# Lightning attention into a SiLU FFN: hand-assigned staging buffers, a 512-column opening FFN, fewer TensorE instructions, and chunks 6 and 7 attended later

## The chip, the cores and the metric

The kernel runs on one core of a Trainium2 chip. The metric is the device time of one execution in microseconds (us). The median of five runs is compared between two versions of the kernel; the profile shows one execution, whose own time is given below. The engines are named PE or TensorE (matmul; its weight loads are shown apart as PEld), DVE or VectorE, ACT or ScalarE, POOL or GpSimd, and SP or SyncE. SyncE issues nearly all DMAs (loads, stores and DMA transposes) from one queue, in the order of the program. TensorE accumulates in PSUM. A tile in PSUM comes from one of four kinds of buffers that the program calls tags: att (3 buffers), h (2), o (2) and kv (1).

## The reference

Inputs are q, k and v of shape (4, 8, 768, 64): four sequences, eight heads, 768 tokens, head size 64; a decay lam per head; and two FFN matrices, w_in (512 x 2048) and w_out (2048 x 512). All are float32. For each head the attention works on blocks of tokens:

```python
intra = (qb @ kb^T) * Dmask            # lam ** (i - j) for i >= j, else 0
out[block] = intra @ vb + (qb * lam ** (pos + 1)) @ kv_state
kv_state = lam ** block * kv_state + (kb * lam ** (block - 1 - pos))^T @ vb
```

The result, seen as 3072 tokens by 512, goes through the FFN:

```python
h = x @ w_in
out = (h / (1 + exp(-h))) @ w_out
```

There is no softmax, so the decay can be split into a factor on q and one on k or v. The output is 3072 x 512 in float32.

## The kernel before, in words

**Tiling.** The 3072 tokens are 24 chunks of 128 tokens, six to a sequence. Matmul operands are bf16. Chunks form ten FFN groups (GROUPS, line 17): five of 256 tokens, four of 384, one of 256. For a chunk c the steps are: scale q and k by the decay; transpose both so that the head dimension lies on partitions; "s", the scores of keys against queries, followed by the causal mask on VectorE (op_m at line 292 for the first chunks, masked at line 479 for the others); "d", the update of the running state kv in PSUM, which is then copied to SBUF as kvbd (copy_kv, line 455); "o", the output from masked scores and values plus state and queries, copied to xt on ScalarE (op_x, line 315; st_o, line 511). When all chunks of a group are in xt, the first FFN matmul runs from xt and w_in into h_ps (lines 529 and 552), ScalarE applies SiLU and writes g, and the second FFN matmul runs from g and w_out into o_ps (line 578). VectorE copies o_ps to ob (line 582) and SyncE stores it (line 570).

**The opening.** Chunks 0 to 3 are handled in pairs (0 and 1, 2 and 3) by a list written out by hand, ORDER (line 25). Each word is a step with its arguments: qc, kc and vc cast and scale half a of the heads (line 257); tq and tk transpose on TensorE (line 264); qt and kt copy the transposes out of PSUM (line 274); s, m, d, kv, o and x are the steps named above; w casts half of a w_in piece; u and g are matmuls and SiLU of the first FFN for groups 0 and 1; wl loads ScalarE's function table; z issues matmuls on a tile of zeros (line 638). The last letter of a word is the engine: D for VectorE, A for ScalarE, P for POOL. Groups 0 and 1 are computed apart, with matmuls of 256 columns; the tokens of a pair are interleaved in xt, and the store of these groups undoes it (line 586).

**Staging.** LOADS (line 23) is the order in which SyncE issues the first loads: halves of K, Q and V of the chunk pairs, then all of w_in. Raw q, k and v pairs and w_out pieces rotate through a pool of six buffers called pair; w_in pieces go through the pools kf, vf and qf, as sixteen transfers of 256 KB (line 161), and are all issued ahead of any cast.

**After the opening.** Lines 674 to 710 mix the second FFN of groups 0 and 1 (down0) with attention of chunks 4 and 5. next_prep (line 662) takes the next chunk: it scales q and k on POOL (lines 356 and 350), issues two DMA transposes on SyncE (qt and kn, lines 373 and 374), and issues the three loads of the chunk two further on (line 232). spread_k copies kn into the block-diagonal tile ktbd on VectorE, spread_v copies the values into vpad (line 387). clear_halves (line 196) zeroes two of these tiles each with four memsets on POOL.

**The stretches.** From group 2 on, stretch (line 745) merges lists of steps by a fractional place: ups(g), the first FFN of group g, spans 0 to 1; pieces(g+1), the attention steps s, d, o of the next group's chunks, spans a given interval; downs(g-1), the second FFN of the group before, likewise. The sorted order is the program order on all engines. Engines run their own instructions in this order and wait for one another by semaphores.

## Time and profile before

| | |
|---|---|
| median of five runs | 217.7 us (216.54 to 220.94) |
| the profiled execution's own time | 216.54 us |
| its span, first to last instruction | 214.8 us |
| TensorE busy | 204.2 us, 95% |
| VectorE busy | 117.5 us, 55% |
| ScalarE busy | 98.5 us, 46% |
| POOL busy | 53.4 us, 25% |
| attention of chunks 0 to 3, until the first FFN matmul | 18.7 us |
| end of the first FFN of groups 0 and 1 | 33.7 us |
| start of group 2's first FFN | 50.9 us |
| mean DMA share, 5 to 60 us / 60 to 105 us / 105 to 155 us | 0.99 / 1.04 / 0.88 |

How to read the lines that follow. A row of a timeline is: start in us from the span's first instruction, time in us of the run of like instructions, engine, line of the kernel, operation, output tile <- input tiles, shape, count, and in brackets the idle time of the engine just before, with what ended it. SPq is SyncE's queue; its rows show the issuing of a transfer, and the landing comes later. Matmuls overlap in the records, so the start-to-start spacing is what one costs: 109 ns at 256 columns and 216 ns at 512. A DMA share is the mean busy share of sixteen DMA engines; it can exceed one where packets queue.

### The profile page before, as it was taken

What the parts mean: (1) busy time and instruction counts of PE and PEld (TensorE: products, weight loads), DVE (VectorE), ACT (ScalarE), POOL (GpSimd) and SP (SyncE); (2) the same over time, 40 slices, a digit from 0 to 9 for tenths busy, and PEclk for the clock granted to TensorE, in tenths of its full rate; (3) what the DMA queues carried; (4) which work ended last, traced back from release to release, by engine and by line L of the source; (5) the groups of instructions that cost most, each with busy time, mean ns of one, the idle gap of its engine ahead of it and who ended that gap; (6) DMA issues with size and microseconds to landing.
All of it is one profiled execution on the core that took longest, in us unless ns stands there. A gap on an engine that the chain in (4) does not pass through costs nothing.

```text
span 214.8 us, 4591 instructions
## 1 busy us (share of the span) xinstructions
PE 204.2 (95%) x1808; PEld 135.7 (63%) x1831; DVE 117.5 (55%) x263; ACT 98.5 (46%) x186; POOL 53.4 (25%) x66
## 2 busy tenths in 40 slices
PE   7878999998699999999999999999999999999994
PEld 5666885565676787766665656556655565566654
DVE  3786447696875599854856785446471352100121
ACT  3983763325362655445555445435445333423210
POOL 6360002539433324323333332222100000000000
PEclk9999999999999999999999999999999999999999
DMA  4999999988899999999999999868411011011112
GB/s 114 332 380 360 371 400 220 318 199 174 214 278 197 228 200 204 176 209 158 194 235 233 226 199 188 200 177 173 123 49 52 2 49 53 0 49 49 52 49 98
DMA packets 95670, 38.58 MB, mean 180 GB/s; under 512 B 81056, under 2 KB 88608, under 8 KB 95648
## 3 DMA queue, kind: packets, MB, share of 16 engines
q1 hardware_dynamic: 95504, 38.29, 71.3%
q8 instruction: 14, 0.23, 0.4%
q14 instruction: 8, 0.07, 0.1%
q10 hardware_dynamic: 144, 0.00, 0.0%
HBM read 27.27 MB, written 6.29 MB: 156 GB/s over the span
## 4 chain that ended last, share of the span: by engine, by line
PE 70%; DMA 14%; SPq 9%; POOL 3%; issue 2%; DVE 1%; DVEq 0%; POOLq 0%
PE o_ps L578 30%; PE h_ps L552 19%; PE h_ps L529 11%; DMA pair<-in_moe_w_out_dram 5%; PE op L507 4%; SPq L224 4%; SPq L232 3%; PE sp L476 3%; DMA vf<-in_moe_w_in_dram 3%; DMA qf<-in_moe_w_in_dram 3%; DMA qf<-in_q_dram 2%; DMA kn<-kb 2%; PE o_part L595 2%; PE kv_ps L452 1%; SPq L161 1%
## 5 line engine op out<-in xcount | busy, mean ns | idle before, releaser
L578 PE MATMUL o_ps<-w_out_bf,g 128*128 128x512 bf16 x345 | 87.8, 379 | 1.2
L578 PEld LDWEIGHTS <-g 128*128 128x128 bf16 x368 | 35.0, 98 | 30.8
L556 ACT ACTIVATE g<-h_ps 128x384 bf16<-128x384 f32 x64 | 31.4, 491 | 46.6 <-PE h_ps L552 46.1
L552 PE MATMUL h_ps<-xt,w_in_bf 128*128 128x384 bf16 x256 | 50.6, 326 | 0.0
L529 PE MATMUL h_ps<-xt,w_in_bf 128*128 128x256 bf16 x384 | 47.2, 273 | 0.7 <-ACT w_in_bf L179 0.7
L534 ACT ACTIVATE g<-h_ps 128x512 bf16<-128x512 f32 x48 | 27.8, 596 | 34.3 <-PE h_ps L529 34.1
L529 PEld LDWEIGHTS <-w_in_bf 128*128 128x128 bf16 x384 | 36.4, 98 | 7.9 <-ACT w_in_bf L179 1.1
L582 DVE COPY ob<-o_ps 128x512 f32<-128x512 f32 x23 | 15.9, 691 | 40.8 <-PE o_ps L578 40.6
L356 POOL TENSOR_TENSOR qb<-qf,lam_fwd 128x512 bf16<-128x512 f32 x18 | 18.9, 1051 | 68.3 <-DMA qf<-in_q_dram 65.0
L552 PEld LDWEIGHTS <-w_in_bf 128*128 128x128 bf16 x256 | 23.7, 98 | 17.2
L483 DVE TENSOR_TENSOR ss<-sp,mask 128x512 bf16<-128x512 f32 (+1 forms) x40 | 21.0, 566 | 12.9 <-PE sp L476 12.6
L387 DVE COPY vpad<-vb 64x256 bf16<-64x256 bf16 x72 | 25.5, 354 | 1.6
L350 POOL TENSOR_TENSOR kb<-kf,lam_bwd 128x512 bf16<-128x512 f32 x20 | 20.9, 1046 | 1.5 <-DMA kf<-in_k_dram 1.4
L183 DVE COPY ktbd<-kn 64x512 bf16<-64x512 bf16 x36 | 14.7, 408 | 10.6 <-DMA kn<-kb 10.3
L183 DVE CAST kvbd<-kv_ps 64x256 bf16<-64x256 f32 x32 | 13.5, 421 | 9.5 <-PE kv_ps L452 9.1
L515 ACT ACTIVATE xt<-op 128x512 bf16<-128x512 f32 x20 | 11.9, 597 | 11.1 <-PE op L507 10.4
L476 PEld LDWEIGHTS <-ktbd 128*128 128x128 bf16 x160 | 9.3, 98 | 6.7 <-DVE ktbd L183 3.8
L476 PE MATMUL sp<-qt,ktbd 128*128 128x128 bf16 (+1 forms) x160 | 10.3, 207 | 2.9 <-DVE ktbd L183 2.9
L179 ACT ACTIVATE vb<-vf 128x512 bf16<-128x512 f32 x18 | 11.2, 622 | 0.0
L507 PE MATMUL op<-ss,vpad 128*128 128x128 bf16 (+1 forms) x160 | 10.3, 207 | 0.0
L507 PEld LDWEIGHTS <-vpad 128*128 128x128 bf16 x160 | 8.9, 98 | 0.3
L183 DVE CAST w_out_bf<-pair 128x1024 bf16<-128x1024 f32 x7 | 5.4, 770 | 5.5 <-DMA pair<-in_moe_w_out_dram 5.5
(83 smaller groups left out, 121.6 us busy)
## 6 DMA issues: line engine op xcount, KB each, us to landing
out_dram<-ob SPq DMA_DIRECT2D x23, 256.0 KB, 3.4
kf<-in_k_dram SPq DMA_DIRECT2D x20, 256.0 KB, 4.0
vf<-in_v_dram SPq DMA_DIRECT2D x20, 256.0 KB, 4.5
qf<-in_q_dram SPq DMA_DIRECT2D x18, 256.0 KB, 3.5
pair<-in_moe_w_out_dram SPq DMA_DIRECT2D x8, 512.0 KB, 8.6
kf<-in_moe_w_in_dram SPq DMA_DIRECT2D x6, 256.0 KB, 5.3
vf<-in_moe_w_in_dram SPq DMA_DIRECT2D x6, 256.0 KB, 5.4
pair<-in_k_dram SPq DMA_DIRECT2D x4, 256.0 KB, 4.5
```

The lines of the kernel that those rows point to most:

```text
L183: nc.vector.tensor_copy(dst, src)
L350: VG[e].tensor_tensor(kb, rawk.pop(c).rearrange("s (p j) d -> s p j d", j=2), decay(lam_bwd, c % NB), op=AL.mult)
L356: nc.gpsimd.tensor_tensor(qb, rawq.pop(c).rearrange("s (p j) d -> s p j d", j=2), decay(lam_fwd, c % NB), op=AL.mult)
L387: nc.vector.tensor_copy(vh[64 * j:64 * j + 64, :, h, j, :], vb[64 * h:64 * h + 64, :, j, :])
L476: nc.tensor.matmul(sp[:, p, :], lhsT=lhsT, rhs=qt[:, p, a:], start=True, stop=True)
L483: VG[e].tensor_tensor(ss, sp, m[:, None, :n].to_broadcast([128, 4, n]), op=AL.mult)
L507: nc.tensor.matmul(dst, lhsT=lhsT, rhs=rhs, start=(i == 0), stop=(i >= len(terms) - NP), skip_group_check=True)
L529: nc.tensor.matmul(hps[g, i][:, a:a + 256], lhsT=w_in_bf[:, ko, m * 128:(m + 1) * 128], rhs=xt[g][:, ko, :], start=(ko == 0 and u == 0), s ...
L534: nc.scalar.activation(gg.rearrange("p u n -> p (u n)"), hps[g, i], AF.Silu)
L552: nc.tensor.matmul(hp[:, a:z], lhsT=w_in_bf[:, ko, m * 128:(m + 1) * 128], rhs=xt[g][:, ko, a:z], start=(ko == 0 and a == 0), stop=(ko == ...
L556: nc.scalar.activation(gg, hp[:, :n], AF.Silu)
L578: nc.tensor.matmul(o, lhsT=gt[g, ko][:, mt * BLK:(mt + 1) * BLK], rhs=w_out_bf[:, ko, :], start=(ko == 0), stop=(ko == KO_OUT - 1))
```

## The change

- **Staging.** Six constant tiles of 512 KB (pairs) are handed out in turn by next_pair, to the K, Q and V pairs of chunks 0 to 3, then to w_in pieces 0 to 5, w_out pieces 0 to 5, q of chunk 4 and w_out pieces 6 and 7. A w_in piece is now one transfer of 512 KB, issued once the casts that read the tile's former content are in the program (the list later); pieces 6 and 7 go through kf and vf. Loads of chunks 4 to 7 are issued after the casts of w_out 0 to 5.
- **Opening order.** ORDER is rewritten: several copies and casts change engines, steps of the second pair are split by halves of the heads, the first FFN block of group 0 starts before the last output step of chunk 3, and zero matmuls fall from 71 to 37 units. A z after the state's tile exists now fills the PSUM tile of the next s, o or u step with zeros.
- **512-column FFN.** The outputs of the first four chunks lie in one tile, xall, in token order. FFN blocks 1 to 3 run both groups at once with matmuls of 512 columns and one SiLU of 512; block 0 keeps 256.
- **Fewer instructions.** op_d multiplies two heads at once: 32 matmuls of 64 rows by 128 columns, where there were 64 of 64 by 64.
- **Layouts.** Halves of the heads come first in the cast tiles; each half has its own PSUM tile in op_o.
- **Chunks 6 and 7.** Their preparations are called one after the other, with the loads of chunks 8 and 9 behind both. In group 2's stretch their attention moves from 0.2-1.15 to 0.8-1.9, the spreading of chunk 6's keys and values to 0.5 and 0.6, chunk 8 is prepared at 0.6, and both output tiles of group 2's second FFN run there, at 1 to 2, where one ran at 1 to 1.5 and the other in the next stretch.

```diff
-LOADS = "K00 Q00 K01 Q01 V00 V01 K20 Q20 K21 Q21 V20 V21 W0 W1 W2 W3 W4 W5 W6 W7"
+LOADS = "K00 Q00 K01 Q01 V00 V01 K20 Q20 K21 Q21 V20 V21"
 ORDER = """
-kc:0,0,A,u z:27 tk:0,0,att qc:0,0,D tq:0,0,h kc:0,1,D,s qt:0,0,D wl z:2 tk:0,1,att kt:0,1,A qc:0,1,P kt:0,0,D vc:0,0,D,s
...
-m:2,1,1,D x:1,0,A m:2,1,0,D x:0,1,A w:0,1,D d:2 kv:2,A z:28 d:3 w:1,0,D o:2,0,o,att w:0,0,A o:2,1 x:2,0,D w:1,1,D w:2,0,D
...
+kc:0,0,D,u z:20 tk:0,0,h qc:0,0,D kt:0,0,A wl z:8 tq:0,0,o kc:0,1,D,s qt:0,0,A z:2 tk:0,1,h qc:0,1,D z:3 tq:0,1,o
...
+kc:2,1,A,u tk:2,1,h qt:2,0,A x:1,1,D x:0,1,D kt:2,1,D vc:2,0,P,s s:2,0,o,h kv:1,A d:2,0 qt:2,1,A vc:2,1,P,s z:2
+s:2,1,att,att m:2,0,0,D m:2,0,1,D kv:2,0,A d:2,1 w:0,1,D kv:2,1,D m:2,1,1,D w:1,1,D o:2,0,h,att m:2,1,0,D w:0,0,A
+u:0,0,0,o,o x:2,0,A d:3 w:1,0,A kv:3,A x:3,0,D u:0,0,1 g:0,0,1 w:2,0,D o:2,1,att,att x:3,1,D x:2,1,A g:0,0,0 w:2,1,D
...
+    pairs = [const.tile([128, 2 * H * D], F32, name=f"pair{i}") for i in range(6)]
+    npair = iter(range(99))
+
+    def next_pair():
+        return pairs[next(npair) % 6]
...
+            t = next_pair().rearrange("p (k f) -> p k f", k=2)
+            nc.sync.dma_start(out=t, in_=(w_in_r if which == "in" else w_out_r)[:, ko, f])
...
-            for p in range(NP):
-                for j in range(2):
-                    nc.tensor.matmul(kv[half[j], p, half[j]], lhsT=kp[c0][half[x], r, 2 * p + j, :],
-                                     rhs=vp[c0][half[x], r, 2 * p + j, :], start=(c == 0 and r == 0 and p == 0), stop=True,
-                                     skip_group_check=True)
+            for p in range(NP) if a is None else (2 * a, 2 * a + 1):
+                hs = slice(2 * (p % 2), 2 * (p % 2) + 2)
+                nc.tensor.matmul(kv[:, p, :], lhsT=kp[c0][half[x], p // 2, r, hs, :], rhs=vp[c0][half[x], p // 2, r, hs, :],
+                                 start=(c == 0 and r == 0 and p == 0), stop=True, skip_group_check=True)
...
+    later = [("in", i, {f"{t}:{b},{a}" for a in range(2)}) for i, (b, t) in enumerate((b, t) for b in (0, 2) for t in ("kc", "qc", "vc"))]
+    later += [("in", 6, set()), ("in", 7, set())] + [("out", i, {f"w:{i},{a}" for a in range(2)}) for i in range(6)]
...
+        ms = (4 * b + 2 * g, 4 * b + 2 * g + 1)
+        for m, tag in zip(ms, tags):
+            hps["m", m] = psum.tile([128, 512], F32, name="h_ps", tag=tag, bufs=2)
+        if h == 0:
+            zeros(hps["m", ms[0]])
+        for m in ms:
+            for ko in range(2 * h, 2 * h + 2):
+                nc.tensor.matmul(hps["m", m], lhsT=w_in_bf[:, ko, m * 128:(m + 1) * 128], rhs=xall[0][:, :, ko, :],
+                                 start=(ko == 0), stop=(ko == KO_IN - 1))
...
+        for _, _, readers in later:
+            readers.discard(name + ":" + ",".join(args.split(",")[:2]))
+        while later and not later[0][2]:
+            load_w(*later.pop(0)[:2])
...
-    def next_prep():
+    def next_prep(load=1):
...
-            if loads:
-                load_c(loads.pop(0))
+            for i in range(load):
+                if loads:
+                    load_c(loads.pop(0))
...
-    next_prep()
+    next_prep(0)
+    next_prep(2)
     down0(3, 0)
     st_o(5)
-    next_prep()
     clear_halves(0, 1)
     down0(3, 1)
...
-    stretch((ups(2), 0, 1), ([(vcast, 6)], 0.0, 0.1), ([(spread_k, 6)], 0.05, 0.05), ([(spread_v, 6)], 0.3, 0.3), (pieces(3), 0.2, 1.15),
-            (downs(2, range(1)), 1, 1.5))
+    stretch((ups(2), 0, 1), ([(vcast, 6)], 0.0, 0.1), ([(spread_k, 6)], 0.5, 0.5), ([(spread_v, 6)], 0.6, 0.6),
+            (pieces(3), 0.8, 1.9), (downs(2, range(2)), 1, 2), ([(next_prep,)], 0.6, 0.6))
     for g in range(3, len(GROUPS)):
         parts = [(ups(g), 0, 1), (pieces(g + 1), *((0.1, 0.95) if g == 3 else (0, 0.85)))]
-        parts.append((downs(g - 1, range(1 if g == 3 else 0, nch[g - 1])), 0, 1))
+        if g > 3:
+            parts.append((downs(g - 1, range(nch[g - 1])), 0, 1))
         stretch(*parts)
```

## The prediction

> **What bounds the kernel now.** First the page: its span and the line of busy times.
>
> ```profile
> span 214.8 us, 4591 instructions
> PE 204.2 (95%) x1808; PEld 135.7 (63%) x1831; DVE 117.5 (55%) x263; ACT 98.5 (46%) x186; POOL 53.4 (25%) x66
> ```
>
> TensorE is idle for 10.6 us in all. Next the waits of all engines: apart from the two ends only one wait of TensorE is over a microsecond. TensorE's order of time shows where it lies, and where the opening ends.
>
> ```profile
> 16.04 1.04 PE L641 MATMUL kv_ps<-zero 128*64 128x64 bf16 x28 [0.86 <-ACT kvbd L179]
> 18.73 2.19 PE L529 MATMUL h_ps<-xt,w_in_bf 128*128 128x256 bf16 x17
> 21.59 12.29 PE L529 MATMUL h_ps<-xt,w_in_bf 128*128 128x256 bf16 x111 [0.67 <-ACT w_in_bf L179]
> ...
> 55.49 0.51 PE L476 MATMUL sp<-qt,ktbd 128*128 128x128 bf16 x8 [2.69 <-DVE ktbd L183]
> 60.27 0.51 PE L476 MATMUL sp<-qt,ktbd 128*128 128x128 bf16 x8 [0.21 <-DVE ktbd L183]
> ...
> 103.12 0.50 PE L476 MATMUL sp<-qt,ktbd 128*128 128x128 bf16 x8
> ```
>
> The reader should see: attention of chunks 0 to 3 until 18.7 us, the opening FFN until 33.7, and then two halts, before the scores of chunk 6 (55.49) and of chunk 7 (60.27). Everything between and after is unbroken. VectorE's order of time says what chunk 6 waited for, and what the later chunks nearly wait for.
>
> ```profile
> 52.22 3.21 DVE L183 COPY ktbd<-kn 64x512 bf16<-64x512 bf16 x2 [0.44 <-DMA kn<-kb]
> 66.18 0.59 DVE L183 COPY ktbd<-kn 64x512 bf16<-64x512 bf16 x2 [2.29 <-DMA kn<-kb]
> 72.81 0.59 DVE L183 COPY ktbd<-kn 64x512 bf16<-64x512 bf16 x2 [1.09 <-DMA kn<-kb]
> 73.43 2.62 DVE L387 COPY vpad<-vb 64x256 bf16<-64x256 bf16 x4
> 78.68 0.58 DVE L183 COPY ktbd<-kn 64x512 bf16<-64x512 bf16 x2
> 102.44 0.59 DVE L183 COPY ktbd<-kn 64x512 bf16<-64x512 bf16 x2 [2.50 <-DMA kn<-kb]
> ```
>
> The pair of copies that takes 0.59 us elsewhere took 3.21 us at 52.22, while POOL ran the four memsets of clear_halves (50.62 to 54.25). The rows at 72.81 and 102.44 matter more: VectorE waits there for the transposed key (kn) of chunks 9 and 14, and TensorE starts the scores of chunk 14 at 103.12, 0.09 us after the copy ends. The slack between key and scores is gone although TensorE does not halt. The last view is SyncE's order of time, the queue that carries all loads, transposes and stores.
>
> ```profile
> 47.64 1.48 SPq L373 DMA_TRANSPOSE qt<-qb  x1
> 49.22 1.22 SPq L374 DMA_TRANSPOSE kn<-kb  x1
> 50.49 0.58 SPq L232 DMA_DIRECT2D qf<-in_q_dram  x1
> ...
> 53.12 0.83 SPq L570 DMA_DIRECT2D out_dram<-ob  x1
> 54.04 1.26 SPq L373 DMA_TRANSPOSE qt<-qb  x1
> 55.40 1.22 SPq L374 DMA_TRANSPOSE kn<-kb  x1
> ...
> 63.25 1.21 SPq L374 DMA_TRANSPOSE kn<-kb  x1
> ```
>
> Each row starts within 0.1 us of the end of the one before it in the full list: from 28 us on SyncE has nearly no free time. It supplies keys at its own pace: kn of chunk 6 is issued at 49.22, that of chunk 14 at 97.67, so 48.45 / 8 = 6.06 us a chunk. TensorE takes scores from chunk 8 (68.35) to chunk 15 (109.22) at 40.87 / 7 = 5.84 us a chunk. So two limits run side by side up to chunk 14: TensorE's own work, and the keys. A gain on one counts only as far as the other follows.
>
> **The change: TensorE's side.**
> Opening. The 28 zero matmuls at 16.04 (1.04 us) go; they stood behind the copy of the state (0.86 us idle), so they covered nothing. Half of group 0's first FFN block moves ahead of the last attention piece. I followed the new order by hand with the durations of before. Early it loses: qt:0,0 goes from VectorE (7.73) to ScalarE, behind a table load that ends at 8.31, so the first scores come at 9.1, not 8.54. After that the two orders run level (scores of chunk 2 near 13.5, before 13.67). The step o:2,0 needs masks that VectorE ends near 15.6 and a state copied near 15.4, so it runs at 15.8, before 17.38. Then 16 FFN matmuls (16 x 109 ns = 1.74 us) fit in, and the FFN is unbroken from about 19.3. That equals a start at 17.55; before it was 18.73 plus 0.67 plus 0.17 of stalls, 19.57. I take 2.0 us; the ends are 0 (the early loss stays) and 3.0 (half of the idle time between 7 and 19 us goes as well). 48 matmuls of 512 columns at 216 ns, the spacing of the o_ps rows, replace 96 of 256 at 109: 10.37 against 10.46, a gain of 0.1.
>
> op_d. 64 matmuls of 64x64 become 32 of 64 rows by 128 columns. Before, 16 of them took 0.44 us (the row at 17.01). After, 8 at the 56 ns of the 128x128 rows take 0.45. Nothing; the ends are -0.2 and +0.4 each, inside the opening's bounds.
> The Trainium skill speaks against this edit. "TensorE: Matmul & The Clock Gate", section "The mechanism", says that a weight load overlaps a running matmul only when its row group differs. All eight of one op_d use the same 64 rows, so their loads (98 ns) would add: 8 x 154 ns = 1.23 us each and 3.1 us for four, an estimate which would leave nothing of the opening's 2.0. The rows of full 128x128 matmuls follow at 56 ns with 98 ns loads, so this case does not bear the rule out for full tiles; no row of before shows 64 rows.
>
> Chunk 6 and 7. Seven of group 2's eight FFN units (0.87 us each) now stand before the scores of chunk 6, where two stood. TensorE therefore reaches them 4.35 us later and finds the copy of 52.22 to 55.43 done: the 2.69 us go, and the 0.21 of chunk 7. Ends 2.0 and 2.9; I take 2.9, because 4.35 exceeds 2.69.
>
> On the way the lead shrinks: the query copies of chunk 4 stand on ScalarE behind the cast of w_out piece 7, which starts when that lands (41.03). The scores of chunk 4, at 43.25 before, cannot come ahead of 42.6. Of the 2.1 us some 1.1 survives, if the transfers come 0.5 us earlier. TensorE's lead after chunk 7 is then about 1.1 + 2.9 = 4.0 us. Group 2's second FFN output tile (4 units, 3.46 us) is now done before group 3 instead of beside it. Chunks 8 and 9 are asked for sooner, and their stretch holds 9.3 us of TensorE work for two chunks against 12.1 us of keys.
>
> **The keys' side.** Staging. w_in pieces 0 to 5 now wait for the casts of K, Q and V. By my chain the last of these waits (vc:2,1 on POOL) ends near 15.3, when three to four pieces of 1.26 us (the spacing at which w_out pieces land) are still queued. w_out pieces wait for the w_in casts, the last near 23, with 3 MB queued. Behind each of these waits stands everything else on SyncE, but the queue holds its cover. Ten transfers instead of sixteen carry w_in, and rates dip in two places (274 GB/s near 18.5, 289 near 24.5, against 400 around them), about 1 us together. I take 0.5 us earlier; ends -1.3 (a piece of 1.26 us missed) and +1.5 (all of the dips and part of one near 35).
>
> Order. Chunk 7's preparation stands before the loads of chunk 8. On POOL nothing moves: the products of chunks 6 and 7 and then the memsets, as before. On SyncE qt and kn of 7 go from 54.04 and 55.40 to 50.5 and 51.8. Chunk 8's three loads go from 50.49 to 53.1, chunk 9's from 56.68 to about 55.3, the store of 53.12 behind them, and then three stores, qt and kn of chunk 8. The number of items is the same. Before, they took 12.8 us from the end of one kn (50.44) to the issue at 63.25. After: two transposes 2.5, six loads and four stores at the spacing at which they land (6 x 0.9 + 4 x 0.67 = 8.1), one transpose 1.25: 11.9 us. I take the difference, 0.9 earlier; ends -0.7 (one store more ahead of the key) and 2.4 (chunk 9's key landing in the median 2.7 us, not its 4.2, as well).
>
> Slack. Chunk 10's scores follow VectorE's chain of 72.81 to 79.26 by 0.05 us; an output copy of 0.69 us leaves that chain, as its unit moves ahead. Chunk 14 had 0.09 us, in a transfer that took 4.7 us against a median of 2.7. So 0 to 2.0 may be used; I take 0.7, the copy.
>
> **Sum.** TensorE would gain 4.0 us, the keys allow 0.5 + 0.9 + 0.7 = 2.1 us; the smaller counts. What is late next is the key of some chunk from 9 to 14. The profiled execution took 216.54 us (214.8 of span and 1.7 around), the lowest of five, 1.16 under their median. It comes to 214.4, and I carry the 2.1 us to the median: 217.7 - 2.1 = 215.6.
>
> **The rivals.**
> All of TensorE's lead arrives. For it: the slow transfer before chunk 14 may be chance, and without it that chunk has 2 us. Against it: chunks 9, 10 and 12 have 0.4, 0.05 and 1.0. Time 217.7 - 4.0 = 213.7.
> The keys come no earlier. For it: SyncE and the transfer engines are busy without a break (share 0.99 between 5 and 60 us), and no edit takes a byte away. Then only slack is gained, 0 to 0.7: 217.3.
> It ends slower, because the queue runs dry at a staging wait in the opening. Place: w_in pieces 3 to 5 or w_out pieces 2 to 4. Price: one for one, as every later transfer shifts. It decides from 2.1 + 1.1 = 3.2 us of dry queue on; four pieces missed are 4 x 1.26 = 5.0 us, so 215.6 + 5.0 = 220.6. Against it: the cover of 3 pieces worked out above.
> The array falls to the slow clock in the opening, where fewer zero matmuls run. In the trace the filler's 256-column matmuls follow at 213 ns until 6.05 and at 109 from then on, and after the 2.69 us halt at 55.49 the spacing is still 109. At the slow pace the attention matmuls between 7 and 15 us, some 5 us of work, take 5 more, and the FFN's first 4.9 us (as long as the filler took to end the slow pace) lose half, 2.4. TensorE leads the keys by 4.0 - 2.1 = 1.9 us, which absorbs as much: 215.6 + 7.4 - 1.9 = 221.1.
> The skill's page on TensorE (section "The HAM clock gate") puts the fall after an idle window of about 3.4 us; no gap in the new order is near that.
>
> **How the numbers follow.** Chances: as forecast 0.45, with its own range 214.1 to 216.6; the whole lead 0.17; no earlier keys 0.20; dry queue 0.12; slow clock 0.06. The half per cent that a measurement of this kernel can tell is 1.1 us. Faster: 0.45 + 0.17 = 0.62; same: 0.20; slower: 0.18. The range goes from 212.8 (a whole lead with 0.9 more from the opening) to 219.2, which leaves out most of the last two cases and little else.
>
> **What would show it.** Right: the 28 zero matmuls gone and the first 512-column FFN matmuls near 21 us; no halt before chunk 6's scores; kn of chunk 8 issued near 61.5, not 63.25; small halts of TensorE (1 to 2 us in all) before scores of chunks 9 to 14, each ended by VectorE's ktbd copy behind a kn transfer. Wrong: op_d's starts 150 ns apart; a transfer share well under 0.9 between 12 and 30 us; matmuls of 256 columns at 213 ns after 8 us; or no halts at all with a gain of 4 us, in which case the keys were not the limit. The forecast fails most easily in the keys' 1.4 us, which rests on spacings and not on a row.

## The result, and the profile after

The changed kernel is not faster: it takes as long as the kernel before to within a quarter of a per cent. Its median is 216.94 us over 35 runs (215.02 to 217.91); that of the kernel before, over 62 runs, is 216.76 us. The ratio is 1.0023, with a 95% interval of 1.0006 to 1.004 (the ratios here leave out disturbed runs, so they can differ a little from the quotient of two medians). The profiled execution of the changed kernel took 215.93 us, against 216.54 of the one that the prediction worked from. So 2.1 us were forecast to go; 0.6 went between the two profiled executions, and none between the medians.

First the page of the changed kernel: its span, its busy times, and the queue that brings TensorE's own instructions, which will matter later.

```profile
span 214.2 us, 4329 instructions
PE 204.2 (95%) x1677; PEld 128.1 (60%) x1700; DVE 112.2 (52%) x267; ACT 98.6 (46%) x185; POOL 53.0 (25%) x65
...
q8 instruction: 13, 0.21, 0.4%
```

TensorE has 131 matmuls fewer, and the same 204.2 us of work. Its order of time (start, duration, line, tiles, and in brackets the idle time ahead with what ended it) shows where it stands still.

```profile
18.27 1.05 PE L544 MATMUL h_ps<-xt,w_in_bf 128*128 128x256 bf16 x8 [0.40 <-ACT w_in_bf L183]
...
20.44 1.91 PE L544 MATMUL h_ps<-xt,w_in_bf 128*128 128x256 bf16 x16 [0.55 <-DVE xt L187]
22.18 10.52 PE L644 MATMUL h_ps<-xt,w_in_bf 128*128 128x512 bf16 x48
33.39 1.46 PE L593 MATMUL o_ps<-w_out_bf,g 128*128 128x512 bf16 x5 [0.69 <-ACT g L653]
...
50.55 6.28 PE L544 MATMUL h_ps<-xt,w_in_bf 128*128 128x256 bf16 x56
56.66 0.50 PE L491 MATMUL sp<-qt,ktbd 128*128 128x128 bf16 x8
...
76.92 0.51 PE L491 MATMUL sp<-qt,ktbd 128*128 128x128 bf16 x8 [1.04 <-DVE ktbd L187]
84.60 0.51 PE L491 MATMUL sp<-qt,ktbd 128*128 128x128 bf16 x8 [1.17 <-DVE ktbd L187]
...
102.57 0.51 PE L491 MATMUL sp<-qt,ktbd 128*128 128x128 bf16 x8
```

The halts before chunks 6 and 7 (2.69 and 0.21 us) are gone: the scores of chunk 6 follow seven FFN units without a gap at 56.66. Two new halts stand at 76.92 and 84.60, before the scores of chunks 10 and 11: 1.04 + 1.17 = 2.2 us. By chunk 14 (102.57, against 103.12 before) only 0.55 us are left, and they stay to the end. VectorE's order of time says that the new halts are late keys, and that the key of chunk 14 was waited for as well.

```profile
76.27 0.59 DVE L187 COPY ktbd<-kn 64x512 bf16<-64x512 bf16 x2 [1.81 <-DMA kn<-kb]
...
83.95 0.59 DVE L187 COPY ktbd<-kn 64x512 bf16<-64x512 bf16 x2 [3.66 <-DMA kn<-kb]
...
101.92 0.59 DVE L187 COPY ktbd<-kn 64x512 bf16<-64x512 bf16 x2 [2.77 <-DMA kn<-kb]
```

SyncE's order of time shows where the keys were late.

```profile
47.25 1.21 SPq L387 DMA_TRANSPOSE kn<-kb  x1
...
56.28 3.64 SPq L585 DMA_DIRECT2D out_dram<-ob  x4
...
61.46 1.20 SPq L387 DMA_TRANSPOSE kn<-kb  x1
...
69.84 2.65 SPq L585 DMA_DIRECT2D out_dram<-ob  x1
72.59 1.22 SPq L386 DMA_TRANSPOSE qt<-qb  x1
73.91 1.22 SPq L387 DMA_TRANSPOSE kn<-kb  x1
...
79.78 1.22 SPq L387 DMA_TRANSPOSE kn<-kb  x1
...
96.94 3.47 SPq L387 DMA_TRANSPOSE kn<-kb  x1
```

The keys of chunks 11 and 14 in the kernel before:

```profile
79.78 1.22 SPq L374 DMA_TRANSPOSE kn<-kb  x1
...
97.67 1.97 SPq L374 DMA_TRANSPOSE kn<-kb  x1
```

The key of chunk 8 is issued at 61.46, 1.8 us earlier than before (63.25). That of chunk 11 is issued at 79.78, the very time of before. Between them lies a store that held SyncE 2.65 us, and the key of chunk 11 then took 4.15 us to land, where the key of chunk 10 took 2.34. The key of chunk 14 is issued 0.73 us earlier than before (96.94 against 97.67), and its copy starts 0.52 us earlier (101.92 against 102.44), which is the 0.55 us that is left.

### The profile page after: what moved, and what is told of

The parts are those of the page before. It is cut to its first block, busy times and chain, and to the rows that moved or that the text cites. A ratio compares the mean times of both kernels' runs of the same rounds, so it can differ in the third digit from the quotient of the medians.

```text
span 214.2 us, 4329 instructions
## 1 busy us (share of the span) xinstructions
PE 204.2 (95%) x1677; PEld 128.1 (60%) x1700; DVE 112.2 (52%) x267; ACT 98.6 (46%) x185; POOL 53.0 (25%) x65
## 4 chain that ended last, share of the span: by engine, by line
PE 51%; DMA 27%; SPq 11%; POOL 6%; issue 2%; DVE 1%; POOLq 0%
PE o_ps L593 23%; PE h_ps L567 18%; DMA qf<-in_q_dram 9%; DMA kf<-in_k_dram 6%; SPq L245 5%; DMA pair<-in_moe_w_out_dram 4%; DMA kf<-in_moe_w_in_dram 4%; PE h_ps L544 3%; SPq L237 3%; PE op L522 3%; DMA kn<-kb 2%; SPq L387 2%; POOL qb L369 2%; DMA pair<-in_q_dram 2%; POOL kb L363 2%
## 5 line engine op out<-in xcount | busy, mean ns | idle before, releaser
L544 PE MATMUL h_ps<-xt,w_in_bf 128*128 128x256 bf16 x288 | 36.0, 273 | 1.0 <-DVE xt L187 0.6
L549 ACT ACTIVATE g<-h_ps 128x512 bf16<-128x512 f32 x36 | 21.4, 597 | 27.7 <-PE h_ps L544 27.5
L567 PEld LDWEIGHTS <-w_in_bf 128*128 128x128 bf16 x256 | 23.7, 98 | 17.2
L544 PEld LDWEIGHTS <-w_in_bf 128*128 128x128 bf16 x288 | 27.1, 98 | 6.5 <-ACT w_in_bf L183 0.6
L363 POOL TENSOR_TENSOR kb<-kf,lam_bwd 128x512 bf16<-128x512 f32 x20 | 21.6, 1081 | 4.7 <-DMA kf<-in_k_dram 4.2
L400 DVE COPY vpad<-vb 64x256 bf16<-64x256 bf16 x72 | 20.5, 285 | 1.6
L187 DVE COPY ktbd<-kn 64x512 bf16<-64x512 bf16 x36 | 12.9, 359 | 13.8 <-DMA kn<-kb 13.5
L187 DVE CAST kvbd<-kv_ps 64x256 bf16<-64x256 f32 (+1 forms) x34 | 14.1, 414 | 10.4 <-PE kv_ps L465 10.1
L530 ACT ACTIVATE xt<-op 128x512 bf16<-128x512 f32 x20 | 11.9, 597 | 16.4 <-PE op L522 15.7
L644 PE MATMUL h_ps<-xt,w_in_bf 128*128 128x512 bf16 x48 | 10.5, 379 | 0.0
```

Of the source, the lines that this page charges most:

```text
L187: nc.vector.tensor_copy(dst, src)
L363: VG[e].tensor_tensor(kb, rawk.pop(c).rearrange("s (p j) d -> s p j d", j=2), decay(lam_bwd, c % NB), op=AL.mult)
L400: nc.vector.tensor_copy(vh[64 * j:64 * j + 64, :, h, j, :], vb[64 * h:64 * h + 64, :, j, :])
L544: nc.tensor.matmul(hps[g, i][:, a:a + 256], lhsT=w_in_bf[:, ko, m * 128:(m + 1) * 128], rhs=xt[g][:, ko, :], start=(ko == 0 and u == 0), s ...
L549: nc.scalar.activation(gg.rearrange("p u n -> p (u n)"), hps[g, i], AF.Silu)
L567: nc.tensor.matmul(hp[:, a:z], lhsT=w_in_bf[:, ko, m * 128:(m + 1) * 128], rhs=xt[g][:, ko, a:z], start=(ko == 0 and a == 0), stop=(ko == ...
```

## The experiments

The theories, as the expectations name them. K: the supply of transposed keys sets the end. T: TensorE's own work and halts set it. D: the new order itself crowds loads or demands together. F (formed after the first four runs): single keys are late because an instruction fetch of TensorE runs beside them; its rival C is that this is chance. All ratios are to the kernel before, with 95% intervals; each run behind the first row stands for 12 executions (late67_shift for 6), beside 29 to 35 of the kernel before on the same chip (11 for late67_shift). Runs on different chips are compared by these ratios.

| run | ratio | 95% interval |
|---|---|---|
| whole change | 1.0023 | 1.0006 to 1.004 |
| late67: only chunks 6 and 7 later | 1.0053 | 1.0016 to 1.0091 |
| opening: only the opening and staging | 0.9973 | 0.9936 to 1.001 |
| late67_oldloads | 1.0006 | 0.9962 to 1.0049 |
| after_oldloads | 0.9976 | 0.9934 to 1.0018 |
| tile2back | 1.0015 | 0.9981 to 1.0049 |
| vact | 1.0007 | 0.9967 to 1.0046 |
| buffers | 0.9986 | 0.9951 to 1.0021 |
| npet8 | 0.9976 | 0.9939 to 1.0013 |
| opening_npet8 | 0.9967 | 0.9934 to 1.0001 |
| opening_npet8_buffers | 0.997 | 0.9948 to 0.9991 |
| opening_npet7_buffers | 0.9927 | 0.989 to 0.9965 |
| shift42 | 0.9979 | 0.993 to 1.0027 |
| shift70 | 1.0058 | 1.0011 to 1.0105 |
| cut42 | 0.9953 | 0.9922 to 0.9983 |
| cut43x4 | 1.0021 | 0.9989 to 1.0054 |
| before_cut42 | 1.004 | 0.9999 to 1.0081 |
| late67_cut40 | 1.0105 | 1.0074 to 1.0136 |
| late67_shift | 1.0167 | 1.0124 to 1.0209 |

### The two halves of the change

late67 takes the kernel before and edits only the place of chunks 6 and 7.

```diff
...
-    next_prep()
+    next_prep(0)
+    next_prep(2)
     down0(3, 0)
     st_o(5)
-    next_prep()
...
-    stretch((ups(2), 0, 1), ([(vcast, 6)], 0.0, 0.1), ([(spread_k, 6)], 0.05, 0.05), ([(spread_v, 6)], 0.3, 0.3), (pieces(3), 0.2, 1.15),
-            (downs(2, range(1)), 1, 1.5))
+    stretch((ups(2), 0, 1), ([(vcast, 6)], 0.0, 0.1), ([(spread_k, 6)], 0.5, 0.5), ([(spread_v, 6)], 0.6, 0.6),
+            (pieces(3), 0.8, 1.9), (downs(2, range(2)), 1, 2), ([(next_prep,)], 0.6, 0.6))
...
```

> The kernel before with the later attention of chunks 6 and 7 alone; its opening, its staging and its matmul forms stay. Theory K (the keys set the end): in both traces the scores of chunk 14 start within 0.1 us after the copy of its key, so the time follows the landing of that key and not TensorE's lead. The halts before chunks 6 and 7 (2.69 and 0.21 us) go, and 2 to 2.5 us of them come back as halts before the scores of chunks 9 to 14. Time 0.2 to 0.6 us under the kernel before. Theory T (TensorE sets the end, and the new opening lost what the later attention won): the 2.9 us stay gone, 2.5 to 2.9 us under the kernel before, some 214.0, with no new halt.

The run called opening undoes exactly these edits in the changed kernel.

> The changed kernel with the attention of chunks 6 and 7 and the preparation of chunk 7 put back where they stood before; the new opening and staging alone. Theory K: the halt before chunk 6 is back, about 2.7 us less what the transfers come earlier (the key of chunk 6 was issued 2.0 us earlier in the changed kernel); keys of chunks 8 to 14 are supplied at the old pace, so the time is within 0.5 us of the kernel before. Theory T with a worse opening: slower than before by 2 us or more, because then the opening's loss stands alone.

Alone, the later attention makes the kernel slower by 0.5%, and the opening makes it faster by 0.3%, the latter within its uncertainty. 1.0053 x 0.9973 = 1.0026, the whole change's 1.0023. Neither theory had the loss. The order of time of TensorE in late67 shows what came for the 2.9 us that went.

```profile
73.68 0.51 PE L476 MATMUL sp<-qt,ktbd 128*128 128x128 bf16 x8 [1.30 <-DVE ktbd L183]
78.79 0.51 PE L476 MATMUL sp<-qt,ktbd 128*128 128x128 bf16 x8 [1.14 <-DVE ktbd L183]
86.14 0.51 PE L476 MATMUL sp<-qt,ktbd 128*128 128x128 bf16 x8 [0.84 <-DVE ktbd L183]
89.45 0.61 PE L507 MATMUL op<-ss,vpad 128*128 128x128 bf16 x8 [0.84 <-DVE ss L483]
```

These are 4.1 us of halts at chunks 9 to 11 (the last one before the output step of chunk 11). The key of chunk 8 is issued at 63.67 here, 0.4 us later than before, not earlier.

### Which part of the later attention costs

tile2back leaves group 2's second output tile where it was, beside group 3's FFN.

```diff
-            (pieces(3), 0.8, 1.9), (downs(2, range(2)), 1, 2), ([(next_prep,)], 0.6, 0.6))
+            (pieces(3), 0.8, 1.9), (downs(2, range(1)), 1, 1.5), ([(next_prep,)], 0.6, 0.6))
...
-        if g > 3:
-            parts.append((downs(g - 1, range(nch[g - 1])), 0, 1))
+        parts.append((downs(g - 1, range(1 if g == 3 else 0, nch[g - 1])), 0, 1))
```

> The changed kernel with the second FFN output tile of group 2 (four units, 3.46 us) put back beside group 3's FFN, so that its store leaves later than the 77.3 us of the changed kernel, behind the keys of chunks 11 and 12. Theory K: the keys of chunks 10 and 11 come up to 1.0 us earlier (the store at 77.31 took 1.05 us of SyncE's time) and their halts (1.04 and 1.17 us) shrink or go; but the same seven stores stand ahead of the key of chunk 14, so the time stays within 0.4 us of the changed kernel, 216.5 to 217.3. Rival D (the demand was merely squeezed together at chunks 8 to 11): the 2.2 us of halts go for good, 214.7.

In the trace the halts before chunks 10 and 11 went, as theory K had it, and others came: 0.72 and 0.69 us behind the scores of chunk 7, 0.28 before those of chunk 14. The key of chunk 11 met no instruction fetch here (these are taken up below) and landed in 2.40 us instead of 4.15, so the place of the store is not shown to be what freed it. 1.0015 is the whole change's ratio within the uncertainty; rival D's 214.7 us would be a ratio of 0.990 (214.7 / 216.76), outside the interval.

The next two keep TensorE's new order and give SyncE its old one: chunk 8's loads ahead of chunk 7's transposes.

```diff
...
-    next_prep(0)
-    next_prep(2)
+    next_prep()
     down0(3, 0)
     st_o(5)
+    next_prep()
```

> The kernel with the later attention of chunks 6 and 7 alone, but with SyncE's old order: the loads of chunk 8 before the transposes of chunk 7, and chunk 9's loads after them. Only TensorE's side of the later attention is left. If SyncE's new order made it slower than the kernel before (six loads and three stores in a row ahead of key 8): 0.5% to 1% of the kernel before's time is won back, ratio to it 0.995 to 1.000. If TensorE's order (group 2's second output tile early, chunks 8 to 11 asked for close together) did: the ratio stays at 1.004 to 1.010.

> The changed kernel with SyncE's old order in the same place, nothing else. If SyncE's new order costs: 0.8 to 1.5 us under the changed kernel, ratio to the kernel before 0.995 to 0.999. If TensorE's order costs: as the changed kernel, 1.001 to 1.004. My prediction had put the new order at 0.9 us of gain; by that this kernel is slower, 1.005 or more.

Both fall by the same 0.47%: 1.0053 to 1.0006 alone, 1.0023 to 0.9976 in the whole. One difference is uncertain by 0.57%, the other by 0.45% (the halves of both intervals, squared, added, and the root); together they give 0.47% with some 0.4%, as both are taken against the same executions of the kernel before and are not wholly independent. So SyncE's new order costs some 1.0 us, from 0.2 to 1.9, and TensorE's new order is worth nothing that can be told. The traces do not show where the 1.0 us lies. With the old order the key of chunk 8 is issued at 61.24 instead of 61.46, and that of chunk 11 at 79.66 instead of 79.78. The profiled executions of both runs (217.79 and 217.97 us) were well above their medians (215.76 and 216.88), so their halts stand for neither. This stays open.

### More keys

vact issues the value loads from chunk 8 on from ScalarE's queue.

```diff
...
-        vraw[c] = load_1(v, c, "vf", 6)
+        vraw[c] = load_1(v, c, "vf", 6, nc.scalar if 8 <= c < 99 else nc.sync)
```

> The changed kernel with the value loads of chunks 8 to 23 issued from ScalarE's queue instead of SyncE's; the bytes are the same. One such row holds SyncE 0.53 to 0.95 us. Theory K, by issue time: SyncE's round of 6.1 us a chunk falls to 5.3, below TensorE's 5.84, the halts before chunks 10, 11 and 14 (1.04, 1.17, 0.08 us) go, and the time is 2.0 to 2.5 us under the changed kernel, near 214.6. Theory K, by transfer volume: the engines that move the data are full (share 1.04 between 60 and 105 us in the kernel before), the keys come no earlier, and the time is within 0.4 us of the changed kernel. Theory T: no change either, and the halts stay.

The keys did come early: that of chunk 14 was issued at 92.95 and landed at 96.69, 5.2 us ahead of the changed kernel's 101.90. The time did not follow. The orders of time of ScalarE and of TensorE in this run, one line of each, show the wait that took the old one's place.

```profile
76.99 0.63 ACT L183 ACTIVATE vb<-vf 128x512 bf16<-128x512 f32 x1 [4.07 <-DMA qf<-in_q_dram]
```

```profile
78.16 0.60 PE L544 MATMUL h_ps<-xt,w_in_bf 128*128 128x256 bf16 x4 [2.69 <-ACT g L549]
```

ScalarE stood for 4.07 us at its own load, which was issued only when a query load of SyncE had landed (issued at 76.50, landing at 76.48). The SiLU behind it came late, its PSUM buffer was not given back, and TensorE halted 2.69 us. So this run does not test whether early keys help.

npet8 and opening_npet8 take four transposes away from SyncE and let TensorE transpose chunks 6 and 7, in the changed kernel and in the opening alone.

```diff
-NPET = 6
+NPET = 8
```

> The changed kernel with queries and keys of chunks 6 and 7 transposed by TensorE instead of by transfers. SyncE loses four transposes of 1.2 to 1.5 us each, so the keys of chunk 8 and later can come up to 5 us earlier; TensorE gets 16 transposes more, 16 x 56 ns = 0.9 us. Theory K (keys set the end): the halts before chunks 10 and 11 (2.2 us) go, and what the opening gained counts; 0.9 - 2.3 = 1.4 us under the changed kernel, near 215.5. Theory T (TensorE sets the end): 0.9 us over it.

> The new opening with the old place of chunks 6 and 7, and their queries and keys transposed by TensorE. Theory K: the halt of 1.38 us before chunk 6 goes with the transfer that it waited for, and the later keys come up to 5 us earlier, so the 0.50 us before chunk 11 and the 0.98 us behind it go too: 2.9 - 0.9 = 2.0 us under the opening alone, near 214.1. If group 2's second output tile beside group 3 matters, this is below the changed kernel with the same transposes by its earlier bunching; theory K with enough keys gives both the same time within 0.5 us.

In the changed kernel this gains 0.47% with some 0.41%, 1.0 us of the 1.4 that K forecast. In the opening alone it gains nothing that can be told (0.9973 to 0.9967), where K forecast 2.0 us. What it removed there is seen when TensorE's halts in the opening alone

```profile
53.80 0.51 PE L491 MATMUL sp<-qt,ktbd 128*128 128x128 bf16 x8 [1.38 <-DVE ktbd L187]
84.35 0.51 PE L491 MATMUL sp<-qt,ktbd 128*128 128x128 bf16 x8 [0.50 <-DVE ktbd L187]
87.63 0.61 PE L522 MATMUL op<-ss,vpad 128*128 128x128 bf16 x8 [0.81 <-DVE ss L498]
```

are set beside the 0.41 and 0.44 us before chunks 6 and 7 that it has in their place: 2.69 against 0.85, less 0.9 of transposes. That leaves 0.9 us in one execution (the spans say 1.1: 214.5 and 213.4), and the ratios show less. So theory K is borne out for the changed kernel by a gain that just clears its uncertainty, and not where the keys have more room.

### The halt at the end of the opening

buffers starts the first FFN output tile on group 0 and closes its FFN units first, so that no PSUM buffer is awaited at 33.39.

```diff
-g:0,2,0 w:7,1,D w:6,1,D u:0,3,0,o,o u:0,3,1 g:0,3,1 u:1,3,0,h,h u:1,3,1 g:1,3,1 g:1,3,0 g:0,3,0
+g:0,2,0 w:7,1,D w:6,1,D u:0,3,0,o,o u:0,3,1 g:0,3,0 g:0,3,1 u:1,3,0,h,h u:1,3,1 g:1,3,0 g:1,3,1
...
-    down0(0, 2, 3, 0, 1)
+    down0(0, 0, 1, 2, 3)
```

> The changed kernel with the halt at the end of its opening taken away: the first FFN output tile starts on group 0 (buffers that group 0's last FFN unit gave back early) instead of group 1, so it need not wait for the last SiLU (0.69 us before 33.39). TensorE leads by 0.7 us more. Theory K (keys set the end up to chunk 14): the halts before chunks 10, 11 and 14 grow by as much, and the time stays within 0.3 us of the changed kernel. Theory T: 0.7 us under it.

> The same edit where keys are in good time: the new opening, the old place of chunks 6 and 7, and their queries and keys transposed by TensorE. There no halt is left behind chunk 7, so TensorE sets the end, and the 0.69 us count in full: 0.5 to 0.8 us under the same kernel without the edit, near 214.8. If something else still sets the end there, no gain.

> The same with chunk 6 alone transposed by TensorE: 8 transposes fewer, 0.45 us of TensorE, but two transposes more on SyncE, some 2.5 us of keys. Theory K: the key of chunk 7 is back on the transfers and halts of about 1 us come back before chunk 7 or chunks 10 to 14, 214.5 to 215.5. If the keys had 2.5 us to spare: 0.45 us under the kernel with both, near 214.4.

The 0.69 us halt is gone in all three. In the changed kernel the ratio falls by 0.0037, uncertain by 0.0039: 0.8 us, from 0 to 1.6, which holds both theories' forecasts. In opening_npet8 it does not fall (0.9967 to 0.997), so a forecast of 0.5 to 0.8 us is not borne out; with an uncertainty of 0.4% it is not excluded either. With chunk 6 alone on TensorE the kernel is clearly faster than both kernels of this study, 0.9927 (0.989 to 0.9965), median 214.68 us. (opening_npet8_buffers, timed beside the same executions, has a median of 214.90, so the two ratios are no measure of the difference between these two.) Its page and TensorE's order of time from 30 us on:

```profile
span 211.4 us, 4338 instructions
...
PE 203.8 (96%) x1684; PEld 128.3 (61%) x1708; DVE 115.1 (54%) x268; ACT 98.5 (47%) x185; POOL 52.8 (25%) x65
```

```profile
53.16 0.51 PE L491 MATMUL sp<-qt,ktbd 128*128 128x128 bf16 x8 [0.48 <-DVE ktbd L187]
```

After 30 us one halt of half a microsecond is left. This profiled execution was the fastest of its run (213.06 us), so it shows what the order can do, not what it mostly does. The run has the old place of chunks 6 and 7, the old order of loads, the new opening, two transposes fewer on SyncE, and no wait for the last SiLU.

### Instruction fetches beside the keys

In the traces the keys of some chunks take 2.4 us to land and others over 4. The late ones have in common that a 16 KB packet of queue q8, TensorE's instructions, starts between 1 us ahead of the issue and the landing. In the nineteen traces whose loads are all on SyncE, between 45 and 130 us, that is so for 78 keys: median 4.11 us, and 73 of them over 3.3 us. Of the 181 others the median is 2.42, and 5 are over 3.3; these five stand beside a packet of q14, another instruction queue. Of the 142 keys beside neither, none took more than 3.0. A late key leaves more time to meet a fetch, but that does not make the difference: counted up to 2.4 us after the issue, whenever the key landed, the figures are 72 of 75 over 3.3, and 6 of 184. In the page above, 0.21 MB of instructions for 1677 matmuls and 1700 weight loads is 62 bytes each, so 16 KB last for some 260 of them, about 14 us. Adding harmless TensorE instructions therefore moves the fetches. shift42 gives the filler's words of 20 and 8 steps a step of 0.5, that is 128 columns; shift70 gives the word of 20 a step of 0.25.

```diff
+        if step < 1:
+            for i in range(int(n / step)):
+                nc.tensor.matmul(dst[:, 0:int(256 * step)], lhsT=zero[:, :BLK], rhs=zero[:, 0:int(256 * step)], start=True, stop=True, skip_group_check=True)
+            return
...
-            fill(wt, n)
+            fill(wt, n, 0.5 if n in (20, 8) else 1)
```

> The changed kernel with its first 28 filler steps cut into 128-column zero matmuls: 42 more TensorE instructions, the same streamed columns, nothing else. It tests what makes single keys late. In five traces the key transposes between 45 and 130 us during which a 16 KB instruction fetch of TensorE ran (queue q8) took a median of 4.25 us to land (20 of them, 3.3 to 5.0), the others 2.43 (50 of them). Theory F (the fetch delays the key): with 84 rows of instructions more in front, each fetch comes a third of a period earlier, 81.2 to about 77.6 and 96.9 to about 91.8, clear of the keys of chunks 11 and 14, which then land 1.5 to 2.4 us earlier; the halt before chunk 11 (1.17 us) goes, and the time is 1.0 to 2.2 us under the changed kernel. Rival C (chance, or the key's own load): the keys of 11 and 14 land as before, within 0.3 us, and the time is the same.

> The same with the first 20 filler steps in 64-column pieces: 70 more TensorE instructions. The control of the other shift. Theory F: the fetches come a little over half a period earlier, 81.2 to about 75.2 and 96.9 to about 88.3; they now meet the keys of chunks 10 (issued near 73.9) and 12 (near 86.2), which land 1.5 to 2 us later, while those of 11 and 14 land earlier; halts before chunks 10 and 12, time within 1 us of the changed kernel and over that of the other shift by 1 us or more. Rival C: the keys land as in the changed kernel.

In shift42 the fetches came at 66.5, 79.0 and 91.1. They met the keys of chunks 9, 11 and 13 (3.44, 3.93, 4.22 us), and that of chunk 14 landed in 2.62 instead of 4.96, 2.35 us earlier. I had expected key 11 to go free as well, and it did not, though the halt before its chunk went (0.22 and 0.37 us were left, before chunks 10 and 12). The time is 0.44% under the changed kernel, uncertain by 0.51%. In shift70 keys 8, 10 and 13 were met (3.76, 3.47, 3.63) and 14 was not (3.13); chunk 10 halted 2.89 us. So which key is late goes with the fetch. The time of shift70 is not the fetches' alone: in five of its twelve executions the granted clock was 0.991 or 0.992, in the profiled one because of a stretch at half clock behind that halt (last section). What the fetches do to the time took a cleaner shift. cut42 leaves the opening alone and cuts the first 42 FFN output matmuls into halves; cut43x4, the control, cuts 43 into quarters, which is one whole fetch more.

```diff
...
-            nc.tensor.matmul(o, lhsT=gt[g, ko][:, mt * BLK:(mt + 1) * BLK], rhs=w_out_bf[:, ko, :],
-                             start=(ko == 0), stop=(ko == KO_OUT - 1))
+            parts = 2 if g < 2 and cut[0] < 42 else 1
+            cut[0] += 1
+            for i in range(parts):
+                cols = slice(i * DM // parts, (i + 1) * DM // parts)
+                nc.tensor.matmul(o[:, cols], lhsT=gt[g, ko][:, mt * BLK:(mt + 1) * BLK], rhs=w_out_bf[:, ko, cols],
+                                 start=(ko == 0 and i == 0), stop=(ko == KO_OUT - 1), skip_group_check=True)
```

> The changed kernel with the first 42 matmuls of its FFN output (33 to 42 us) cut into halves of 256 columns: 42 more TensorE instructions (84 rows with their weight loads), the same columns, and nothing touched in the opening. Theory F: instruction fetches come near 66, 78 and 92 us instead of 70.3, 81.2 and 96.9; the key of chunk 14 lands within 2.8 us instead of 4.96, a key of chunk 9 or 13, which have slack, is caught instead, and the time is 0.5 to 2.0 us under the changed kernel (the earlier shift gave about 1.0). Rival C (the fetches do not matter): key 14 takes over 4 us as before, and the time is the same within 0.4 us.

> The control: 43 of those matmuls cut into quarters of 128 columns, 129 instructions or 258 rows more, which is one fetch of 16 KB (256 rows). The fetches fall where they fell in the changed kernel, 70, 81 and 97 us, with one more in front; the pieces cost 43 x (4 x 56 - 216) ns = 0.3 us of TensorE. Theory F: the keys of chunks 11 and 14 are slow again (4 us and more), and the time is that of the changed kernel within 0.5 us. If merely having more and smaller instructions makes the kernel faster, it gains as the other cut does.

The transfers of the 2 us around the issue of chunk 14's key, in the changed kernel, in cut42 and in cut43x4 (queue, packets, MB, share; then issues with the median us to landing):

```profile
q14 instruction: 1, 0.01, 6.2%
q8 instruction: 1, 0.02, 3.3%
...
kn<-kb SPq DMA_TRANSPOSE x1, 5.0
```

```profile
q14 instruction: 1, 0.01, 1.0%
...
kn<-kb SPq DMA_TRANSPOSE x1, 2.8
```

```profile
q14 instruction: 1, 0.01, 4.8%
q8 instruction: 1, 0.02, 2.8%
...
kn<-kb SPq DMA_TRANSPOSE x1, 4.4
```

With the fetch of q8 beside it the key takes 5.0 and 4.4 us, without it 2.8; a packet of q14 is there in all three. cut42 is 0.70% faster than the changed kernel, uncertain by 0.35% (1.5 us), and the control, with three times as many added instructions, is equal to it (1.0021). The two cuts were timed side by side, and their medians (214.76 and 216.22 us) differ by 1.46 us. Of this the smaller pieces of the control cost some 0.36 us: the scores of chunk 6 start at 57.08 in its trace, at 56.72 in that of cut42. So the times speak for theory F, that the place of the fetches moves the time of this kernel. The two profiled executions do not show how. In that of cut42 the key of chunk 11 still took 4.28 us, the halts were 1.22 and 0.87 us, and its 215.38 us lie above its median. In that of the control the copy of key 14 ended 0.54 us before the scores of chunk 14 began (101.65 and 102.19), so the late key held nothing up, and its 215.51 us lie under its median. The lateness of single keys is shown by the transfers and the gain by the times; that the one makes the other is argued, not shown.

Would it help any of these kernels? The same cuts in the kernel before and in late67:

> The kernel before with the first 42 matmuls of its FFN output cut into halves, as in the changed kernel's cut that gained 0.7%. In its trace the fetches at 70.4 and 97.6 us met the keys of chunks 9 and 14, whose slack was 0.42 and 0.0 us. Theory F in general (the place of the fetches is worth 1 to 1.5 us to any of these kernels): fetches near 66, 80 and 93, key 14 within 2.8 us, time 0.5 to 1.5 us under the kernel before; then comparing two kernels with the fetches in one place each says little of the change. Theory F for the changed kernel alone: TensorE of the kernel before halts nowhere after chunk 7, so the time is within 0.4 us of it.

> The kernel with the later attention of chunks 6 and 7 alone, with 40 matmuls of its FFN output cut into halves, in place of the shift by the filler, which slowed TensorE's clock in the opening and left the fetches at 71.0 and 83.7 us, on the keys. Theory F: fetches near 66, 78.5 and 94 instead of 70.0, 82.4 and 98.4; keys of chunks 9 and 11 land within 2.8 us (4.33 and 4.11 before), at least 2 of the 4.3 us of halts at chunks 9 to 12 go, and the time is 1.2 to 2.6 us under 218.16. Rival D (bunched by the order itself): halts of 4.3 us within 1 us, time within 0.6 us of 218.16.

Not as forecast. The kernel before does not gain (1.004, 0.9999 to 1.0081). The ratio of late67 rises by 0.52%, uncertain by 0.49%, where F forecast 1.2 to 2.6 us of gain. In both the fetches fell on the keys of chunks 9, 11 and 13 (4.50, 4.52, 4.12 and 3.87, 3.79, 4.38 us) and left 14 free (3.22 and 2.47): moving fetches off one key puts them on others.

The profiled execution of late67_cut40 fits neither theory. It is the fastest of its twelve (215.62 us against a median of 217.60), and its view of waits shows no halt of TensorE between 50 and 130 us, though the keys of chunks 9 and 11 are late. TensorE reached the scores of chunk 6 at 59.36, 2.45 us later than in late67 (56.91), after its clock had fallen in the opening (last section), and the keys of chunks 8 to 11 landed 1.1 to 2.3 us earlier than in late67. So the 4.1 us of halts are no fixed property of this order, and one trace of it is not all of them. That the fetches cause the loss of late67 is not shown; the order of the loads is its likelier cause, by the runs above.

late67_shift was to test the same by the filler.

```diff
-                nc.tensor.matmul(wt[:, 0:2], lhsT=zero[:, :BLK], rhs=zero, start=True, stop=True)
+                for _ in range(2):
+                    nc.tensor.matmul(wt[:, 0:1], lhsT=zero[:, :BLK], rhs=zero[:, :BLK], start=True, stop=True)
```

> The kernel with the later attention of chunks 6 and 7 alone, and its first 34 zero matmuls of 256 columns cut into halves: 34 more TensorE instructions, the same columns. In its trace instruction fetches at 70.0, 82.4 and 98.4 us met the keys of chunks 9, 11 and 14, which took 4.33, 4.11 and 3.58 us to land, and TensorE halted 1.30, 1.14, 0.84 and some 1.0 us around the scores of chunks 9 to 12. Theory F (fetches of TensorE's instructions delay those keys, and that made this kernel slower than the kernel before): the fetches come near 66.5, 79 and 94, the keys of chunks 9 and 11 land within 2.7 us, at least 2 us of the halts go, and the time is 1.2 to 2.6 us under that kernel's 218.16. Rival D (the loads and keys are bunched by the new order itself, wherever the fetches fall): the halts stay within 1 us of 4.3 in sum, and the time within 0.6 us of 218.16.

It says nothing of F: the fetches came at 71.0 and 83.7, on the same keys. TensorE's clock fell in the opening instead, which the last section shows.

## Why the prediction was wrong, point by point

The step that failed is the keys' 2.1 us: a lead of the key of chunk 8 was counted as a lead of all keys behind it. At chunk 14 it came to 0.52. The steps in order.

The opening. Right: the 28 zero matmuls went; the 48 wide matmuls took 10.52 us, 216 ns each and the last one's tail; op_d cost nothing. The last op_d of the changed kernel, and that of the kernel before:

```profile
17.25 0.62 PE L343 MATMUL kv_ps<-vp,kp 64*128 64x128 bf16 x8
```

```profile
17.01 0.44 PE L330 MATMUL kv_ps<-vp,kp 64*64 64x64 bf16 x16
```

The 32 matmuls of the new op_d start 55 or 56 ns apart within a run (the eight at 17.25 take 0.62 us: some seven steps of 56 ns, and one matmul of 0.22). So the estimate of 154 ns from the Trainium skill's page "TensorE: Matmul & The Clock Gate", section "The mechanism", does not hold for 64-row weights here. The kernel before had shown as much, against what I wrote: its op_d also loads weights of 64 rows, all in the same half of the rows, and 16 of them took 0.44 us.

Wrong: the 2.0 us. The FFN's equivalent start, worked back from its first wide matmul, is 22.18 - 32 x 109 ns = 18.69. The same from before's 33.72 is 33.72 - 128 x 109 ns = 19.77. So 1.1 came, because TensorE waits 0.40 and 0.55 us between the FFN units that I had taken as unbroken from 19.3. Most of that was lost again at 33.39: the first output tile wants a PSUM buffer of the last FFN unit and waits 0.69 us for its SiLU, and the last matmul's tail of 0.15 us is no longer covered. With the 0.1 of the wide matmuls the output tiles start 0.33 us earlier than before, not 2.0. I had followed the masks and states by hand to the FFN's start, and not the buffers to its end.

Chunks 6 and 7. Right, to the size: 2.9 us of halts went. With the 0.33 that is a lead of 3.2, where I had 4.0. At chunk 10 the trace has it: its scores start 2.39 us earlier than before after a halt of 1.04, 3.4 together.

The keys. The forecast rested on this term, 0.5 + 0.9 + 0.7 = 2.1 us. The sign named for the first two came: the key of chunk 8 was issued at 61.46, where I had said near 61.5. But that was luck, as two errors met in it. Staging was worth more than I gave it: the key of chunk 6 is issued 2.0 us earlier (47.25 against 49.22), beyond my upper end of 1.5. The order on SyncE, which I put at 0.9 us of gain, is a loss: from the end of the issue of key 6 to the issue of key 8 it takes 13.0 us (48.46 to 61.46), where my sum had 11.9 and the kernel before 12.8, and the runs that gave the old order back put its whole cost at about 1.0 us. My sum took each row at the spacing at which transfers land, the four stores at 0.67 us each, 2.7 in all; they held SyncE 3.64 us (from 56.28), which is most of the difference. And the lead did not last: the key of chunk 11 was issued at the time of before, behind a store that held SyncE 2.65 us, and the copy of chunk 14's key came 0.52 us earlier. The slack of 0.7 was not to be had: the scores of chunks 10, 11 and 14 follow the copy of their key by 0.06 us.

That the smaller of two counts sets the gain. The form was right, and in the profiled executions so is the size once the 0.52 stands for the 2.1: TensorE gains 0.55. The removed halts came back before scores of chunks 9 to 14, each ended by the key's copy, 2.3 us in sum where I had said 1 to 2. The rival "the keys come no earlier", at 217.3 and 0.20, named the outcome, though keys 8 and 9 came 1.8 us earlier; that lead was gone at the issue of key 11, and TensorE's was 1.06 us at the scores of chunk 11 (84.60 against 85.66) and 0.55 at those of chunk 14. I took a mean pace of 6.06 us a chunk. The pace is not even: a key beside an instruction fetch takes 1.7 us longer, and the chunk that meets one can become the one that binds.

The other rivals. No staging wait ran dry: the transfer share between 12 and 30 us is 1.05, as before. The clock did not fall in the new opening: the granted clock of all 36 executions of the changed kernel on record is 0.998 or more.

The level. The five runs that I started from had a median of 217.7; with 62 it is 216.76, 0.9 lower. So the forecast of 215.6 is only 1.3 us under the result, while the change itself was missed by more: 2.1 us of gain foretold, and 0.5 of loss (0.0023 x 216.76) measured. That the time lies so near the forecast is luck. The two profiled executions still differ by 0.6 us of gain, so some 1.1 us lie between these two and the medians, and what makes them up stays open.

## What to carry to other kernels

A halt that ends with a late transfer is not removed by doing other work first: ask for the next deadline on the same queue, chunk by chunk, and count the gain only up to the first one that has no slack. Change the order on the issuing queue in a run of its own; here it cost some 1.0 us, and the version with the new opening, the old order, two transfers fewer and no wait for the last SiLU took 0.7% less than the kernel before. When two versions differ by half a per cent, look where the instruction fetches fall, and shift them with a few harmless instructions before the difference is laid to the change; a control shifted by one whole fetch tells whether the shift was the cause. And profile more than one execution, or compare the profiled one with the median first: here several of them were not typical of their run.

## What the hardware showed that I had not expected

Instruction fetches of TensorE share the transfer engines with the data. One 16 KB packet takes about 1.06 us of one engine (3.3% of 16 engines in 2.0 us, in the lines above), and the key transposes beside it land in a median of 4.1 us instead of 2.4 (78 and 181 of them). Why they lose 1.7 us to 1.06 us of one engine is not shown.

TensorE's clock fell in the old opening in two of its six traces, at 18.7 us in late67_cut40, where nothing of the opening was edited, and at 18.6 in late67_shift. None of the fourteen traces with the new opening shows that. TensorE's clock and busy time in late67_cut40, stretch by stretch (us, PE busy, granted clock, transfer share, GB/s), and ahead of it the halts of its opening:

```profile
16.17 0.38 PE L330 MATMUL kv_ps<-vp,kp 64*64 64x64 bf16 x12 [1.40 <-POOL vp L253]
17.40 1.04 PE L647 MATMUL kv_ps<-zero 128*64 128x64 bf16 x28 [0.86 <-ACT kvbd L179]
```

```profile
17.00:18.50 1.50, 1.10 (x36) 1.00 1.03 371
18.50:20.00 1.50, 1.50 (x38) 0.55 0.97 298
20.00:22.00 2.00, 2.00 (x25) 0.50 1.04 384
22.00:23.50 1.50, 1.50 (x14) 0.98 1.09 389
```

Here two halts of 1.40 and 0.86 us with work between them came ahead of the half clock, while after one of 2.69 us in the kernel before the clock stayed full. In shift70 a halt of 2.89 us was followed by the half clock as well, from 81.1 for 3.4 us. The Trainium skill's page "TensorE: Matmul & The Clock Gate" (section "The HAM clock gate") states the fall for at least one idle window of about 3.4 us, free-running. The length of the low stretch (3.4 us in all three) agrees with the window; that the window must be wholly idle does not, as no halt of 3.4 us stands ahead of any of them. The old opening can thus lose some 1.7 us of TensorE's work, half of 3.4, in one execution and not in another; the new opening was free of it in these traces. The granted clock of single executions agrees: it was under 0.995 in 48 of the 168 of the kernel before that the record lists, and in none of the 36 of the changed kernel. Where in those 48 it fell is not on record; half the clock for 3.4 us of 214 would show as 0.992, and most of them have 0.991 or 0.992. I had looked for that danger only in the new one.
